# Two of the three weight loads that open the kernel, moved from SyncE's DMA queue to ScalarE's

## The chip, the cores and the metric

The kernel runs on one core of one Trainium2 chip. The metric is the device time of one execution in microseconds. Three runs of the kernel before took 254.72, 254.77 and 254.78 us; the median, 254.77 us, is the time that the prediction starts from.

## The reference

Two attention blocks with 32 heads of width 20 are computed on separate inputs, and their outputs stand side by side. Both inputs x have 2048 rows of 640 columns in bf16. A is a sliding-window softmax attention over the last 256 keys, B is a linear attention.

```
qkv = x @ wqkv                       # 640 x 1920: columns of q, of k, of v
A:  scores = q @ k.T * 20 ** -0.5, kept where 0 <= i - j < 256
    o = softmax(scores) @ v;  out[..., :640] = o @ wo
B:  pq, pk = phi(q), phi(k);  phi(t) = (t + 1 if t > 0 else exp(t)) + 1e-6
    kv = pk.T @ v;  z = sum of pk over rows;  o = (pq @ kv) / (pq @ z + 1e-6)
    out[..., 640:] = o @ wo
```

## The kernel before, in words

The 2048 rows are cut into 4 stretches of 512 (SB), each stretch into 4 blocks of 128 (TPS), and the 640 columns into 5 chunks of 128 (KT). A's projections q, k and v of stretch 0 are computed in an opening; then a long loop over the score tiles of A runs, into which a plan written out by hand (lists of due times) fills the matmuls of the later projections, of B and of the output products. The order of instructions on each engine is fixed by the order in which the program issues them (`manual_schedule`); an engine that waits holds up all that stands behind it on that engine.

The change lies in the opening. The first stretch of A's x is not transposed by a DMA. Its rows are loaded as they are into a tile named phi: block 0, block 1, and then blocks 2 and 3 together (`load`, L172 and L173). TensorE turns each block through an identity (`transposes`, L178) into PSUM tiles named first, and DVE (even blocks) or ScalarE (odd blocks) copies the result to xA (L352, L349). The weight columns of v are loaded in three parts along the contraction: chunk 0, chunks 1 and 2, chunks 3 and 4 (`v_parts`, L968), each chunk 160 KB. `v_abreast` then works on all eight products of v (four blocks by two halves) side by side: chunk 0 for the four products of blocks 0 and 1, then the transposes of blocks 2 and 3, then chunk 0 for the other four, then chunks 1 and 2 for all eight, then chunks 3 and 4 (matmuls L411). The raw weight columns of q and k (tiles qpad and kpad, L334, 800 KB each) are regrouped by DVE, ScalarE and GpSimd (`regroup`) into wqk, from which the q rows are computed (L276).

Before any of this is there, TensorE runs dummy products on a zeroed tile (`warm_up`, L196): 18 at once, and 2 more between the transposes of block 0 and those of block 1.

Every load of the kernel before is issued by SyncE (nc.sync), one after the other: block 0, block 1, v chunk 0, blocks 2 and 3, v chunks 1 and 2, v chunks 3 and 4, raw q, raw k, the transposed second stretch of x (xA, L163), B's k weights (wB, L157), and B's first stretch (xB, L163). ScalarE issues no DMA.

Of the kernel before, what the change touches and what calls it, by code (L numbers as in the profile page):

```python
# [21 lines left out]
TPS = SB // P  # L22
# [70 lines left out]
def kernel(  # L93
# [10 lines left out]
    nc = tc.nc  # L104
    _, S, D = A_x.shape
# [35 lines left out]
    w_sb = {}  # L141
# [19 lines left out]
    def load_x(n, s):  # L161
        t = xp.tile([P, KT, SB], BF16, name=f"x{n}")
        nc.sync.dma_start_transpose(out=t[:], in_=xsrc[n][s * SB : (s + 1) * SB, :])  # L163
        return t

    def load_x_first():

        tok = pqp.tile([P, TPS, D], BF16, name="phi")
        src = xsrc["A"][0:SB, :].rearrange("(t p) d -> p t d", p=P)
        t = xp.tile([P, KT, SB], BF16, name="xA")  # L170

        def load(t0, t1):  # L172
            nc.sync.dma_start(out=tok[:, t0:t1, :], in_=src[:, t0:t1, :])  # L173

        def transposes(tb):
            ps = first_ps.tile([P, 2 * SB], BF16, name="first")
            for c in range(KT):
                nc.tensor.transpose(  # L178
                    ps[:, c * P : (c + 1) * P], tok[:, tb, c * P : (c + 1) * P], ident[:]
                )  # L180
            dst = t[:, :, tb * P : (tb + 1) * P]
            pv = ps[:, 0:D].rearrange("p (c q) -> p c q", q=P)

            for c in (slice(0, 2), slice(2, KT)):
                (act_copy if tb % 2 else dve_copy)(dst[:, c, :], pv[:, c, :])

        return t, load, transposes

    def warm_up(wait):

        z = op.tile([P, TPS, D], BF16, name="osb")
        nc.vector.memset(z[:, 0, 0:P], 0.0)
        ps = dps.tile([P, SB], F32, name="dense")
        for n in wait:
            for _ in range(n):
                nc.tensor.matmul(  # L196
                    ps[:, 0:P], lhsT=z[:, 0, 0:P], rhs=z[:, 0, 0:P], start=True, stop=True
                )
            yield
# [45 lines left out]
    load = {"A": 0, "D": 0}  # L245
# [82 lines left out]
    def load_raw(i):  # L328

        pl, name = ((qp, "qpad"), (kp, "kpad"))[i]  # L330
        t = pl.tile([P, NG, SB], BF16, name=name)
        raw = t.rearrange("p g q -> p (g q)")[:, 0 : KT * D].rearrange("p (k n) -> p k n", n=D)
        wv = A_wqkv.rearrange("(kt p) n -> p kt n", p=P)
        nc.sync.dma_start(out=raw, in_=wv[:, :, i * D : (i + 1) * D])  # L334
        return raw
# [12 lines left out]
    def act_copy(dst, src):  # L348
        nc.scalar.activation(out=dst, in_=src, func=ACT.Copy)  # L349
# [610 lines left out]

    v_parts = ((0, 1), (1, 3), (3, KT))
    wv = A_wqkv.rearrange("(kt p) n -> p kt n", p=P)
    load_tokens(0, 1)
    load_tokens(1, 2)
    for k0, k1 in v_parts:
        if k0 == 1:
            load_tokens(2, TPS)
        nc.sync.dma_start(out=w_sb["A"][:, k0:k1, :], in_=wv[:, k0:k1, 2 * D : 3 * D])  # L968
    raw = [load_raw(i) for i in range(2)]
    xA[1] = load_x("A", 1)  # L970
    load_w("B", B_wqkv, 1, nc.sync)
    xB[0] = load_x("B", 0)
    dummies = warm_up((18, 2))
    for tb in range(2):
        next(dummies)
        transposes(tb)
    v_tok[0] = v_bufs[0]
    for i, _ in enumerate(v_abreast(xA[0], v_tok[0], by_tokens, v_parts)):
        if i == 3:
# [191 lines left out]
```

## Time and profile before

The profiled execution took 255.21 us, of which the span from the first to the last instruction is 253.5 us; the median of the runs shown is 254.77 us, 0.44 us below the profiled one.

| what | value |
|---|---|
| TensorE matmul busy | 242.4 us, 96% of the span |
| ScalarE busy | 196.8 us, 78% |
| GpSimd busy | 186.3 us, 73% |
| VectorE busy | 169.5 us, 67% |
| DMA | 37.04 MB, all of the kernel's own transfers on one queue (q1) |

Times in the profile's rows are microseconds from the start of the span. SPq is SyncE's sequencer issuing DMAs; a DMA's row in a timeline is the time that its issue takes and not that of the transfer. In a chain of waits, a row of a DMA reaches from its issue to its landing.

### The profile page before, as it was taken

How to read it: one execution, taken by the hardware profiler on the slowest of the kernel's cores; microseconds unless marked ns; L12 is line 12 of the kernel's file. 1: busy time of each engine (PE TensorE's matmuls, PEld its weight loads, DVE VectorE, ACT ScalarE, POOL GpSimd, SP SyncE). 2: the span in 40 equal slices, each digit the busy share in tenths (PEclk: the TensorE clock that was granted, in tenths of full speed). 3: DMA queues.
4: the chain of work that ended last, by engine and by line, in shares of the span. 5: the costliest groups of instructions: out<-in, count | busy, mean ns of one | idle time of the engine just before them, and what ended most of it. 6: DMA issues, size and time to landing. Idle time of an engine off the chain costs nothing.

```text
span 253.5 us, 8721 instructions
## 1 busy us (share of the span) xinstructions
PE 242.4 (96%) x3677; PEld 141.2 (56%) x3723; DVE 169.5 (67%) x311; ACT 196.8 (78%) x194; POOL 186.3 (73%) x310
## 2 busy tenths in 40 slices
PE   7999999999999999999999999999999999999994
PEld 5644446556755546457445555556455465655573
DVE  1264777767754565767664867677889779859662
ACT  3366788898767788997657888889988899999541
POOL 1125798878787798687778969889877978999800
PEclk9999999999999999999999999999999999999999
DMA  6997699897764252994559495525969956494614
GB/s 195 329 263 152 113 188 109 104 288 192 98 119 28 44 193 41 226 291 127 88 106 185 110 199 117 140 34 86 186 104 171 182 89 168 93 181 101 193 58 153
DMA packets 68396, 37.04 MB, mean 146 GB/s; under 512 B 51589, under 2 KB 67333, under 8 KB 68357
## 3 DMA queue, kind: packets, MB, share of 16 engines
q1 hardware_dynamic: 68357, 36.49, 68.5%
q8 instruction: 29, 0.48, 0.7%
q14 instruction: 10, 0.08, 0.1%
HBM read 14.42 MB, written 9.83 MB: 96 GB/s over the span
## 4 chain that ended last, share of the span: by engine, by line
PE 80%; ACT 6%; issue 5%; DVE 4%; DMA 2%; POOL 1%; SPq 0%; ACTq 0%
PE dense L276 46%; PE S_ps L784 10%; PE dense L559 8%; PE dense L831 7%; PE dense L411 5%; ACT p L792 4%; DMA phi<-in_A_x_dram 2%; ACT e L286 1%; DVE phi L293 1%; PE first L411 1%; POOL p L807 1%; PE dense L713 1%; DVE e L290 1%; DVE tok L749 1%; PE dense L642 1%
## 5 line engine op out<-in xcount | busy, mean ns | idle before, releaser
L807 POOL TENSOR_SCALAR_AFFINE_SELECT p<-p 128x256 bf16<-128x256 bf16 (+2 forms) x280 | 176.5, 660 | 43.3 <-ACT p L792 41.8
L792 ACT ACTIVATE p<-S_ps 128x2048 bf16<-128x2048 f32 x76 | 142.9, 1880 | 33.6 <-PE S_ps L784 29.4
L276 PE MATMUL dense<-xA,wqk 128*128 128x512 bf16 x188 | 48.9, 380 | 1.4 <-issue 1.0
L784 PEld LDWEIGHTS <-kpad 20*128 20x128 bf16 (+1 forms) x1216 | 21.9, 98 | 29.5 <-issue 25.5
L784 PE MATMUL S_ps<-qpad,kpad 20*65 20x64 bf16 (+3 forms) x1216 | 33.7, 227 | 0.3
L844 DVE STREAM_TRANSPOSE T<-dense 128x512 f32<-128x512 f32 x32 | 22.8, 713 | 15.7 <-PE dense L831 15.3
L290 DVE TENSOR_SCALAR e<-e 128x512 bf16<-128x512 bf16 x40 | 18.4, 459 | 20.5 <-ACT e L286 20.5
L293 DVE SCALAR_TENSOR_TENSOR phi<-dense,e 128x512 bf16<-128x512 f32 x40 | 27.7, 692 | 1.6
L276 PEld LDWEIGHTS <-wqk 128*128 128x128 bf16 x200 | 17.9, 98 | 19.2
L831 PE MATMUL dense<-p,vA 128*32 128x64 bf16 (+2 forms) x1216 | 25.9, 231 | 0.6 <-ACT osb L261 0.4
L276 PE MATMUL dense<-wB,xB 128*128 128x128 bf16 (+1 forms) x155 | 25.3, 297 | 0.5 <-issue 0.3
L276 PE MATMUL dense<-xB,wB 128*128 128x512 bf16 x90 | 24.6, 380 | 0.6 <-issue 0.3
L276 PE MATMUL dense<-wo,oT 128*128 128x512 bf16 (+4 forms) x161 | 24.5, 293 | 0.6 <-DVE phi L293 0.3
L559 PE MATMUL dense<-tok,phi 128*128 128x129 bf16 (+1 forms) x152 | 24.1, 296 | 0.9 <-issue 0.8
L286 ACT ACTIVATE e<-dense 128x512 bf16<-128x512 f32 x40 | 23.6, 600 | 1.4 <-PE dense L276 0.8
L411 PE MATMUL dense<-wA,xA 128*128 128x320 bf16 x140 | 24.0, 304 | 0.2 <-issue 0.2
L276 PE MATMUL dense<-wB,xA 128*128 128x128 bf16 (+1 forms) x153 | 22.9, 296 | 0.6 <-issue 0.5
L831 PEld LDWEIGHTS <-vA 128*32 128x32 bf16 x1216 | 19.4, 97 | 4.2 <-issue 1.3
L261 ACT ACTIVATE osb<-dense 128x512 bf16<-128x512 f32 (+2 forms) x28 | 15.8, 578 | 5.7 <-PE dense L276 5.5
L411 PEld LDWEIGHTS <-xA 128*128 128x128 bf16 x160 | 14.9, 98 | 8.5 <-ACT xA L349 0.8
L749 DVE TENSOR_TENSOR tok<-tok,rden 128x640 bf16<-128x640 bf16 x16 | 18.3, 1141 | 0.2 <-issue 0.2
L861 DVE TENSOR_TENSOR N<-T,recA 128x320 bf16<-128x320 f32 (+1 forms) x28 | 16.1, 574 | 3.4 <-DMA oT<-N 2.5
(66 smaller groups left out, 196.8 us busy)
## 6 DMA issues: line engine op xcount, KB each, us to landing
out_dram<-osb SPq DMA_DIRECT2D x7, 640.0 KB
x_scr<-xB SPq DMA_DIRECT2D x4, 640.0 KB
tok<-in_B_x_dram SPq DMA_DIRECT2D x4, 640.0 KB
xB<-x_scr SPq DMA_DIRECT2D x4, 640.0 KB
wB<-in_B_wqkv_dram SPq DMA_DIRECT2D x3, 800.0 KB
q_scr<-qpad SPq DMA_DIRECT2D x16, 60.0 KB
k_scr<-kpad SPq DMA_DIRECT2D x16, 60.0 KB
qpad<-q_scr SPq DMA_DIRECT2D x16, 60.0 KB
```

The lines of the kernel that those rows point to most:

```text
L276: nc.tensor.matmul(dst, lhsT=lhs(kt), rhs=rhs(kt), start=(kt == 0), stop=(kt == KT - 1))
L286: nc.scalar.activation(out=view(e), in_=src, func=ACT.Exp)
L290: nc.vector.tensor_scalar(out=e[:], in0=e[:], scalar1=1e-6, scalar2=1.0 + 1e-6, op0=ALU.add, op1=ALU.min)
L293: nc.vector.scalar_tensor_tensor(out=dst, in0=src, scalar=0.0, in1=view(e), op0=ALU.max, op1=ALU.add)
L411: nc.tensor.matmul(ps[:, 0 : hh * DH], lhsT=xt[:, kt, tb * P : (tb + 1) * P], rhs=w_sb["A"][:, kt, i * hh * DH : (i + 1) * hh * DH], start ...
L559: nc.tensor.matmul(out, lhsT=pk[:, tb, c * P : (c + 1) * P], rhs=x[:, tb, lo:hi], start=(i == 0), stop=(i == len(blocks) - 1),)
L749: nc.vector.tensor_tensor(out=vh, in0=vh, in1=rden_of[s][:, tb, :, :].to_broadcast([P, H, DH]), op=ALU.mult)
L784: nc.tensor.matmul(S_ps[0:keys, j, col : col + n], lhsT=k_pad[kb // TPS][rows, g, ko : ko + keys], rhs=q_pad[s][rows, g, q0 : q0 + n], sta ...
L792: nc.scalar.activation(out=p, in_=S_ps[:], func=ACT.Exp, scale=scale)
L807: nc.gpsimd.affine_select(out=dst, in_=v, pattern=[[0, 4], [0, n], [sgn, w]], compare_op=ALU.is_ge, fill=0.0, base=base, channel_multiplie ...
L831: nc.tensor.matmul(O_ps[32 * j : 32 * (j + 1), q0 : q0 + n], lhsT=v_flat[kb // TPS % 3][:, at + j * HV : at + j * HV + 32], rhs=p[:, j, co ...
L844: nc.vector.transpose(out=T.rearrange("p b e -> p (b e)"), in_=O_ps[:])
```

## The change

The loads of v's chunks 1 and 2 and of chunks 3 and 4 are issued by ScalarE (nc.scalar) and no longer by SyncE. SyncE issues block 0, block 1, v chunk 0, blocks 2 and 3, and then at once raw q, raw k and the rest in the order they had. Ahead of ScalarE's two DMAs stands a copy of one element per partition within the zeroed tile (`act_copy(z[:, 1, 0:1], z[:, 0, 0:1])`), and ahead of that copy ScalarE's function table load. `warm_up`, which holds the copy, is started ahead of the loads in the program; the order of instructions on TensorE and on VectorE is the same as before. `load` takes the issuing engine as an argument, and gets nc.sync each time.

```diff
-        def load(t0, t1):
-            nc.sync.dma_start(out=tok[:, t0:t1, :], in_=src[:, t0:t1, :])
+        def load(t0, t1, eng):
+            eng.dma_start(out=tok[:, t0:t1, :], in_=src[:, t0:t1, :])
...
         nc.vector.memset(z[:, 0, 0:P], 0.0)
+        act_copy(z[:, 1, 0:1], z[:, 0, 0:1])
...
-    load_tokens(0, 1)
-    load_tokens(1, 2)
-    for k0, k1 in v_parts:
-        if k0 == 1:
-            load_tokens(2, TPS)
-        nc.sync.dma_start(out=w_sb["A"][:, k0:k1, :], in_=wv[:, k0:k1, 2 * D : 3 * D])
+    def load_v(part, eng):
+        k0, k1 = part
+        eng.dma_start(out=w_sb["A"][:, k0:k1, :], in_=wv[:, k0:k1, 2 * D : 3 * D])
+
+    dummies = warm_up((18, 2))
+    next(dummies)
+    load_tokens(0, 1, nc.sync)
+    load_tokens(1, 2, nc.sync)
+    load_v(v_parts[0], nc.sync)
+    load_tokens(2, TPS, nc.sync)
+
+    load_v(v_parts[1], nc.scalar)
+    load_v(v_parts[2], nc.scalar)
     raw = [load_raw(i) for i in range(2)]
     xA[1] = load_x("A", 1)
     load_w("B", B_wqkv, 1, nc.sync)
     xB[0] = load_x("B", 0)
-    dummies = warm_up((18, 2))
-    for tb in range(2):
-        next(dummies)
-        transposes(tb)
+    transposes(0)
+    next(dummies)
+    transposes(1)
```

## The prediction

> **What bounds the kernel now.** First the page: the busy times and the chain that ended last say which engine carries the end.
>
> ```profile
> PE 242.4 (96%) x3677; PEld 141.2 (56%) x3723; DVE 169.5 (67%) x311; ACT 196.8 (78%) x194; POOL 186.3 (73%) x310
> PE 80%; ACT 6%; issue 5%; DVE 4%; DMA 2%; POOL 1%; SPq 0%; ACTq 0%
> ```
>
> TensorE is the bound: 96% busy, 80% of the chain. DMA has 2% of the chain, about 4.3 us, and all of it is one transfer. The chain in order of time shows which:
>
> ```profile
> 2.19 4.26 DMA phi<-in_A_x_dram
> 6.45 0.05 issue
> 6.50 0.75 PE first L178 x10
> 7.25 0.02 issue
> 7.27 0.77 ACT xA L349 x2
> 8.04 0.04 issue
> 8.08 0.30 PE first L411
> ```
>
> So the start hangs on blocks 2 and 3 of x: issued at 2.19, landed at 6.45. The transposes and ScalarE's copies follow, and from 8.08 TensorE runs without a hole. In the waits of TensorE after 8.1 us there is no DMA at all; the longest single one is 0.4 us (ScalarE's copy of an output). What the landing loses or gains is therefore handed to the end one for one. The timeline shows what TensorE and the two issuing engines do around it:
>
> ```profile
> 0.80 1.28 ACT L349 ACT_TABLE_LOAD   x1 [0.80 <-PEq L1155]
> 2.19 0.43 SPq L173 DMA_DIRECT2D phi<-in_A_x_dram  x1
> 2.66 0.98 SPq L968 DMA_DIRECT2D wA<-in_A_wqkv_dram  x2
> 4.25 1.40 PE L411 MATMUL dense<-wA,xA 128*128 128x320 bf16 x4
> 4.49 0.77 ACT L349 ACTIVATE xA<-first 128x256 bf16<-128x256 bf16 x2 [2.40 <-PE first L178]
> 6.50 0.73 PE L178 MATMUL first<-ident,phi 128*128 128x128 bf16 x10 [0.86 <-DMA phi<-in_A_x_dram]
> ```
>
> TensorE has done its last piece at 5.64 and stands for 0.86 us. The loads that are moved are issued right behind the one it waits for. Last, the windows of one microsecond, for the DMA (last two columns: busy share of the 16 engines, GB/s):
>
> ```profile
> 2.00:3.00 1.00, 1.00 (x12) 0.91 (x10) 0.00 (x0) 0.09 (x1) 0.00 (x0) 1.00 0.93 273
> 3.00:4.00 1.00, 1.00 (x12) 0.93 (x11) 0.26 (x2) 0.00 (x0) 0.00 (x0) 1.00 0.96 224
> 4.00:5.00 1.00, 1.00 (x8) 0.47 (x6) 0.29 (x2) 0.51 (x2) 0.00 (x0) 1.00 0.77 232
> 5.00:6.00 1.00, 0.64 (x2) 0.05 (x2) 0.00 (x0) 0.25 (x1) 0.00 (x0) 1.00 0.98 338
> 6.00:7.00 1.00, 0.50 (x9) 0.51 (x10) 0.01 (x1) 0.00 (x0) 0.00 (x0) 1.00 1.08 350
> 7.00:8.00 1.00, 0.89 (x8) 0.28 (x5) 0.54 (x2) 0.73 (x2) 0.00 (x0) 1.00 0.96 326
> 8.00:9.00 1.00, 0.93 (x8) 0.68 (x7) 0.00 (x0) 0.03 (x1) 0.00 (x0) 1.00 1.05 385
> ```
>
> The DMA engines are busy almost throughout: the opening is short of bandwidth, not of issues. With 0.033 MB before 2.0, the bytes moved by 3, 4, 5, 6, 7, 8 and 9 us are 0.306, 0.530, 0.762, 1.100, 1.450, 1.776 and 2.161 MB. In the order of issue the loads end at these sums: block 0 0.164, block 1 0.328, v chunk 0 0.492, blocks 2 and 3 0.819, v chunks 1 and 2 1.147, v chunks 3 and 4 1.475, raw q 2.294, raw k 3.113. The sum 0.819 is passed at 5.17 us, and the load lands at 6.45: 1.28 later, since the slowest of the 16 engines decides. For raw q it is 9.37 against 10.41, where GpSimd's wait for it ends: 1.04 later. A landing is thus the time of its sum plus 1.0 to 1.3 us.
>
> **The change part by part.** *The copy of one element* on ScalarE starts after the table load, at 2.08. The nearest rows are its smallest copies of the opening, 0.33 us (128x160). ScalarE had nothing to do until 4.49. *The two DMAs* cost ScalarE what SyncE paid, 0.98 us, so about 2.4 to 3.4: done before 4.49, cost nothing. If they ended after 4.49, the copies of block 1 would be late, and behind them the third and fourth v product; these are covered by TensorE's wait for blocks 2 and 3.
>
> *SyncE* loses two issues. The issue of blocks 2 and 3 stays at 2.19: nothing in front of it has gone. Behind it, raw q moves from 3.69 to 2.66, raw k from 4.20 to 3.18, the transposing load of xA from 4.77 to 3.74, and wB's and xB's follow if the line of bytes lets them. This gains nothing on the path: raw q is passed at the sum 2.294 with the same bytes ahead of it, and wB and xB, issued at 12.79 and 13.42, meet their first user on TensorE only at 28.0.
>
> *The order of the bytes* is the real edit. Before, 0.819 MB go first, and v's 0.655 MB stand behind them on the one queue. Now v's parts stand at the head of a second queue and are worked off beside the first. SyncE's first issue at 0.81 brings bytes at about 1.8, 1.0 later; so ScalarE's at 2.4 brings them at 3.4, when 0.396 MB are moved and 0.423 MB of SyncE's remain up to the end of blocks 2 and 3. The trace has one queue only, so how two share the engines has no row. The ends: SyncE's queue keeps its place (nothing goes ahead, +0, and with the lag of raw q in place of 1.28 even -0.24); or all of v goes ahead: the sum to pass is 1.474, at 7.07, and +1.9. I take equal shares, as both queues ask the same busy engines all the time: 0.423 of v's go with 0.423 of SyncE's, the sum to pass is 1.242, at 6.41, and with raw q's lag of 1.04 (one DMA in a steady stream, as this will be) blocks 2 and 3 land at 7.45, 1.0 us later. With the old lag it is 1.24.
>
> [...]
>
> *What else moves with it.* v chunk 0 shares too: 0.096 MB of it are left at 3.4, the sum 0.588 is passed 0.42 later, and the four products at 4.25 end by 6.06 and not 5.64: hidden, as the wait reaches to 7.45. v chunks 1 and 2 pass at about 6.4 at the latest and land by 7.7; TensorE asks for them after the four chunk 0 products of blocks 2 and 3, then at 9.2 (8.22 plus 1.0). v chunks 3 and 4: all 0.655 MB shared, sum 1.706, passed at 7.8, landed by 9.1; asked for at 11.4. Raw q lands at 10.4 as before, and DVE takes it up behind v's products, at 11.8 plus 1.0. All hidden.
>
> The sum: +1.0 on the landing, 0 for the rest. In the profiled execution of before, 255.21 us (span 253.5), that makes 256.2; against the median of the runs, 254.77, which is 0.44 lower, **255.8 us**. Shares from equal to most to v, and lags of 1.04 to 1.28, make the likeliest case 255.4 to 256.4.
>
> **The rivals.**
>
> *A: v's loads come too late to matter much.* Condition: ScalarE's issue starts not at 2.4 but towards 4. For it: ScalarE's next row after the table load is at 4.49, so the trace doesn't show how soon it is free; against: nothing stands between. With an issue at 3.8, bytes come at 4.8, when 0.716 MB are moved and 0.103 remain; the sum 0.922 is passed at 5.47, +0.3, a little more where slow engines have more left: about +0.4, 255.2, within 0.2%. The same place is reached if the engines stay with SyncE's queue (+0).
> [...]
>
> *B: faster, since a second queue fills the slack of the engines.* Place: the windows from 3 to 5 us, where they move 224 and 232 GB/s and later 338 to 385. If those are waits of single transfers that another queue's can fill, the rate from 3.4 on is 385: with equal shares 0.846 MB take 2.2 us, to 5.6, and if the lag, then no longer made by stalls, is 0.3, the landing is at 5.9, 0.55 earlier: 254.2. The turning point: share and rate together must bring it ahead of 6.45, that is a lag under 0.85 even at full rate. TensorE's own work up to 5.64 caps the gain at 0.86 (253.9). Against it: busy shares of 0.96 and 0.77 in these windows leave little to fill.
>
> *C: TensorE falls back to its slow pace.* It did 5 transposes in 0.71 us at 2.99 and 10 in 0.73 at 6.50. Its hole would grow from 0.86 to about 1.8 us, and what comes behind could run at the early pace for a microsecond or two: +1.0 more, 256.8. Against it: after the hole of 0.86 it was at full pace.
>
> *D: nothing changes* beyond the issuing queue, as every load of v is hidden before and after: covered by A's +0.
>
> **How the numbers follow.** 0.2% is 0.51 us, about what a measurement of this kernel can tell from no change. The forecast has 0.58 (255.4 to 256.4), C and other large losses 0.07, A and D 0.16, B 0.19. Slower by over 0.2% takes the forecast and C: 0.65; within it A and D and the mild end of B: 0.17; faster the rest of B: 0.18. For 8 in 10 the range runs from the middle of B's 253.9 to 254.26, about 254.1, to the forecast's upper end, 256.4.
>
> **What the profile after will show.** ScalarE's two issues at about 2.4 to 3.4 (A: near 4). A second hardware queue with 0.66 MB. The chain's DMA row ending at about 7.45 and not 6.45, the ten transposes at 7.5, and TensorE without a hole from about 9.1, every later row about 1.0 later. The waits of TensorE still with blocks 2 and 3, now 1.5 to 1.8 us, and none for v. The prediction is wrong if those blocks land before 6.9 (then look at the rates from 3 to 5 us, B, or at a late issue, A), or if TensorE waits for v's parts or raw q, which would mean that the second queue is served far less than half.

## The result and the profile after

The changed kernel takes 257.0 us (median of 6 runs, 256.61 to 257.51) against 254.78 us for the kernel before (median of 6 runs, 254.72 to 255.97). The ratio is 1.0064, with a 95% interval of 1.0038 to 1.0091. So it is slower, by 2.2 us by the medians and by 1.6 us by the ratio. The forecast was 255.8 us with a range of 254.1 to 256.4: the direction was right, the size was not, and the time lies above the range. The changed kernel was run twice more, on other chips, with 1.0063 and 1.0071. The profiled execution shown here took 256.73 us, with a span of 255.0 us (before: 253.5).

The page of the profile after: busy times, the DMA queues (packets, MB, share of the 16 engines' span), and the chain that ended last.

```profile
PE 248.0 (97%) x3723; PEld 141.4 (55%) x3723; DVE 168.1 (66%) x311; ACT 196.9 (77%) x195; POOL 186.8 (73%) x310
q1 hardware_dynamic: 67813, 35.83, 65.7%
q10 hardware_dynamic: 544, 0.66, 0.8%
PE 88%; DVE 3%; ACT 3%; DMA 2%; issue 2%; SPq 0%; POOL 0%; ACTq 0%
```

TensorE is still the bound. There is a second hardware queue, q10, with v's 0.66 MB, as the diff says. The chain in order of time (start, length, what):

```profile
2.19 4.92 DMA phi<-in_A_x_dram
7.11 0.05 issue
7.15 1.04 PE first L178 x10
8.19 1.28 PE first L412 x4
9.47 1.82 PE dense L412 x8
...
14.55 5.40 PE dense L277 x25
```

The same pieces in the chain of before:

```profile
8.38 1.09 PE dense L411 x8
...
12.73 0.22 PE dense L276
```

Blocks 2 and 3 of x land at 7.11, 0.66 later than before (6.45). But the first q product, the last row, stands at 14.55, and before it was at 12.73: 1.82 later. So the landing is only the smaller part of the loss. The chain shows the rest: the ten transposes take 1.04 (0.75 before) and the eight v products 1.82 (1.09 before), with no wait between. The timeline shows ScalarE and TensorE (in brackets the idle time before, and what ended it):

```profile
0.80 1.28 ACT L350 ACT_TABLE_LOAD   x1 [0.80 <-PEq L1162]
1.04 0.95 ACTq L966 DMA_DIRECT2D wA<-in_A_wqkv_dram  x2
2.10 0.20 ACT L350 ACTIVATE osb<-osb 128x1 bf16<-128x1 bf16 x1
...
4.90 0.45 PE L178 MATMUL first<-ident,phi 128*128 128x128 bf16 x5 [0.82 <-DMA phi<-in_A_x_dram]
6.25 0.70 PE L412 MATMUL dense<-wA,xA 128*128 128x320 bf16 x4 [0.90 <-DMA wA<-in_A_wqkv_dram]
7.15 1.04 PE L178 MATMUL first<-ident,phi 128*128 128x128 bf16 x10 [0.20 <-DMA phi<-in_A_x_dram]
...
9.26 2.03 PE L412 MATMUL dense<-wA,xA 128*128 128x320 bf16 x8
```

Two things are to be seen. First, ScalarE issues its two DMAs from 1.04 on (the single rows start at 1.04 and 1.51), in the midst of the table load of 0.80 to 2.08 and ahead of the one-element copy at 2.10, which stands before them in the program. So v's 0.66 MB do not come in behind the x blocks, but among the very first of them. In the window from 3 to 4 us the two queues moved (packets, MB, share of the 16 engines):

```profile
q10 hardware_dynamic: 228, 0.27, 76.0%
q1 hardware_dynamic: 63, 0.08, 21.7%
```

From 2.75 to 3.5 us it was 141 packets of ScalarE's queue and 1 of SyncE's: block 0 was through, and v's chunks 1 and 2, issued at 1.04, went ahead of block 1, issued at 1.25. Second, TensorE now has three waits in place of one: 0.82 for block 1, 0.90 for v chunk 0, 0.20 for blocks 2 and 3. The landings, each the last of the 16 engines, from the semaphore events of the two traces:

| load | before | after |
|---|---|---|
| block 0 | 2.94 | 3.11 |
| block 1 | 3.68 | 4.85 |
| v chunk 0 | 4.18 | 6.21 |
| blocks 2 and 3 | 6.45 | 7.11 |
| v chunks 1 and 2 | 7.28 | 4.42 |
| v chunks 3 and 4 | 8.11 | 6.11 |
| raw q | 10.36 | 9.42 |
| raw k | 12.58 | 11.64 |

What TensorE needs first comes later, and what it needs last comes earlier. After the change the landings follow the order of issue over both queues: block 0 (0.81), v chunks 1 and 2 (1.04), block 1 (1.25), v chunks 3 and 4 (1.51), v chunk 0 (1.72), blocks 2 and 3 (2.19). The windows of one microsecond (busy time of PE, PEld, DVE, ACT, POOL, which are TensorE's matmuls and weight loads, VectorE, ScalarE and GpSimd, with the number of instructions; then TensorE's granted clock as a share of full speed, the DMA share and GB/s):

```profile
3.00:4.00 1.00, 1.00 (x9) 0.67 (x7) 0.09 (x1) 0.00 (x0) 0.00 (x0) 1.00 0.98 352
4.00:5.00 1.00, 0.18 (x3) 0.11 (x3) 0.46 (x2) 0.00 (x0) 0.00 (x0) 1.00 1.06 376
5.00:6.00 1.00, 0.35 (x5) 0.23 (x5) 0.00 (x0) 0.61 (x2) 0.00 (x0) 1.00 1.07 387
...
7.00:8.00 1.00, 0.85 (x10) 0.77 (x10) 0.31 (x2) 0.00 (x0) 0.00 (x0) 0.71 1.07 366
8.00:9.00 1.00, 1.00 (x5) 0.26 (x4) 0.25 (x1) 0.77 (x2) 0.00 (x0) 0.50 1.08 367
9.00:10.00 1.00, 1.00 (x5) 0.56 (x4) 0.00 (x0) 0.00 (x0) 0.53 (x3) 0.50 1.08 369
10.00:11.00 1.00, 1.00 (x7) 0.56 (x5) 0.00 (x0) 0.00 (x0) 0.58 (x3) 0.58 1.08 342
```

The engines move more than before from 3 to 6 us (352, 376, 387 GB/s against 224, 232, 338). And TensorE's granted clock falls to 0.50: in the trace from 7.43 to 10.84, which is 3.41 us. The hole of 4 to 7 us lies ahead of the fall (TensorE busy for 0.18, 0.35 and 0.70 us of its three windows), and the slow pace comes just when the data is there: five products in each of the windows 8:9 and 9:10, where before there were eight and ten matmuls. The second of these windows before:

```profile
9.00:10.00 1.00, 1.00 (x10) 0.70 (x8) 0.00 (x0) 0.00 (x0) 0.00 (x0) 1.00 1.05 362
```

How the loss is made up in this pair of traces, by the starts of the same weight loads on TensorE: +0.65 at the transposes of blocks 2 and 3, +1.04 at the first of the eight v products at 9.26, growing to +1.82 at the last of them; 0.30 of it is given back between 57 and 66 us, and the spans differ by 1.5.

### The profile page after: what moved, and what is told of

It is laid out like the page before. It is cut to its first block, busy times and chain, and to the rows that moved or that the text cites. A ratio compares the mean times of both kernels' runs of the same rounds, so it can differ in the third digit from the quotient of the medians.

```text
span 255.0 us, 8768 instructions
## 1 busy us (share of the span) xinstructions
PE 248.0 (97%) x3723; PEld 141.4 (55%) x3723; DVE 168.1 (66%) x311; ACT 196.9 (77%) x195; POOL 186.8 (73%) x310
## 4 chain that ended last, share of the span: by engine, by line
PE 88%; DVE 3%; ACT 3%; DMA 2%; issue 2%; SPq 0%; POOL 0%; ACTq 0%
PE dense L277 49%; PE S_ps L785 10%; PE dense L560 9%; PE dense L832 8%; PE dense L412 7%; DMA phi<-in_A_x_dram 2%; ACT p L793 2%; PE first L412 1%; PE dense L714 1%; DVE phi L294 1%; ACT e L287 1%; DVE tok L750 1%; PE dense L643 1%; PE dense L671 1%; ACT osb L262 1%
## 5 line engine op out<-in xcount | busy, mean ns | idle before, releaser
L277 PE MATMUL dense<-xA,wqk 128*128 128x512 bf16 x200 | 50.9, 380 | 0.0
L277 PEld LDWEIGHTS <-wqk 128*128 128x128 bf16 x200 | 17.9, 98 | 19.2
L277 PE MATMUL dense<-xB,wB 128*128 128x512 bf16 x100 | 26.1, 380 | 0.0
L277 PE MATMUL dense<-wB,xB 128*128 128x512 bf16 (+1 forms) x160 | 25.9, 300 | 0.0
L560 PE MATMUL dense<-tok,phi 128*128 128x129 bf16 (+1 forms) x160 | 25.5, 300 | 0.0
L277 PE MATMUL dense<-wo,oT 128*128 128x512 bf16 (+4 forms) x165 | 24.9, 295 | 0.3 <-DVE phi L294 0.3
L277 PE MATMUL dense<-wB,xA 128*128 128x512 bf16 (+1 forms) x160 | 24.1, 299 | 0.0
L277 PEld LDWEIGHTS <-oT 128*128 128x128 bf16 x165 | 13.2, 98 | 8.4 <-issue 0.7
```

The lines of the kernel that those rows point to most:

```text
L277: nc.tensor.matmul(dst, lhsT=lhs(kt), rhs=rhs(kt), start=(kt == 0), stop=(kt == KT - 1))
L560: nc.tensor.matmul(out, lhsT=pk[:, tb, c * P : (c + 1) * P], rhs=x[:, tb, lo:hi], start=(i == 0), stop=(i == len(blocks) - 1),)
```

## The experiments

The questions: is it the place of v's loads in the line of bytes, and their early issue, or the copy and the new order of the program; and how much of the loss is the landing, and how much the pace? All times are medians; "before" is the kernel before on the same chip. One number helps to read all of them, the start of the first q product (the first piece of `dense` L277 in the chain), since the spans follow it:

| run | first q product | span | difference |
|---|---|---|---|
| before | 12.73 | 253.5 | 240.8 |
| after | 14.55 | 255.0 | 240.5 |
| after_again | 14.54 | 255.0 | 240.5 |
| after_third | 14.69 | 255.2 | 240.5 |
| e1_held | 15.97 | 256.9 | 240.9 |
| e1_again | 15.71 | 256.2 | 240.5 |
| e2_more_dummies | 13.69 | 254.2 | 240.5 |
| e2_again | 13.54 | 254.0 | 240.5 |
| e3_last_part | 13.45 | 254.5 | 241.0 |
| e4_blocks | 13.65 | 254.1 | 240.4 |
| e4_again | 12.25 | 252.9 | 240.6 |
| e5_all_sync | 12.49 | 252.9 | 240.4 |
| e7_blocks_dummies | 12.59 | 253.0 | 240.4 |
| e9_few_dummies | 11.75 | 252.2 | 240.4 |

Over 4 us of difference in the opening, the rest of the kernel takes 240.4 to 241.0 us. So nearly all of the difference is made in the opening.

### e1_held and e1_again: ScalarE's issue held behind the copy

The copy writes one column of the tile that the DMA fills, so that the program has the DMA wait for it; in the run the copy ends at 2.31 and the issue starts at 2.33. This is the kernel that the forecast had in mind.

```diff
-        act_copy(z[:, 1, 0:1], z[:, 0, 0:1])
+        act_copy(w_sb["A"][:, 1, 0:1], z[:, 0, 0:1])
```

> ScalarE's two loads are now really held behind the table load: the one-element copy writes into the place that the first of them fills, so they are issued at about 2.35 and not at 1.04. Theory E (they went too early: 0.66 MB shared the engines with every one of SyncE's opening loads, and the holes that this made in TensorE's work put it back to half pace from 7.4 to 10.8): v's bytes start at about 3.4, blocks 2 and 3 have to wait for a sum of 1.24 MB, which at the 370 GB/s that the two queues moved together is passed at 5.7 and lands at about 6.4; block 1 lands at 3.7, v chunk 0 before 4.7; TensorE has no hole over 1 us and keeps its full pace: 254.6 to 255.0 us. Rival F (the forecast's sum: what counts is that v goes ahead of blocks 2 and 3 at all): landing at 7.45, 255.8 us.

Measured: 258.7 us (256.16 to 259.52) against 255.25, ratio 1.0119 (1.0080 to 1.0159). The timeline of e1_held:

```profile
2.10 0.21 ACT L350 ACTIVATE wA<-osb 128x1 bf16<-128x1 bf16 x1
2.33 0.94 ACTq L966 DMA_DIRECT2D wA<-in_A_wqkv_dram  x2
...
8.10 0.73 PE L178 MATMUL first<-ident,phi 128*128 128x128 bf16 x10 [1.75 <-DMA phi<-in_A_x_dram]
```

The issue now starts at 2.33, where the forecast had put it. Block 1 is back at 3.56, v chunk 0 at 5.08. Yet blocks 2 and 3 land at 8.05, later than in the changed kernel, and TensorE waits 1.75 us for them. Both theories missed: holding the issue does not give the time back, and the forecast's own premise does not give the forecast's time. The DMA records and the semaphore events show where. ScalarE's first bytes move at 4.02, 1.69 after its issue and not the 1.0 of the forecast, and by 5 us its queue has moved 0.03 MB. SyncE's queue has moved 0.819 MB, the sum up to blocks 2 and 3, by 6.08, with 0.27 MB of v beside it, where the forecast had 0.423 of v and 6.41. Of the 16 engines, the middle one had its part of blocks 2 and 3 in at 6.20 (5.54 before), the last at 8.05. So the share cost less than was forecast; it is the slowest engine that lies 1.85 behind the middle one, where the forecast had a lag of 1.04 behind the sum. After the hole the clock was at half from 9.65 to 13.06.

Was the late engine chance? The same kernel again, on another chip:

> The held issue once more, since its first profile had the landing of the last of 16 engines at 8.05, 1.85 after their median (6.20). Theory J (equal shares for each engine, and one straggling engine decides, which differs from run to run): median again at about 6.2, last anywhere from 6.6 to 8.1, and times that scatter over 2 us or more, from 255 to 259. Rival K (a second queue that opens while blocks 2 and 3 are under way always slows them like that): last at 7.9 to 8.2 and 258 to 259 us again.

Measured: 257.87 us (257.12 to 259.65) against 255.21, ratio 1.0107 (1.0070 to 1.0145). Blocks 2 and 3 land at 8.27, the middle engine at 6.07; half clock from 8.50 to 11.91. So both traces of this order of issue have the late engine. Why one engine was 1.85 and 2.20 us behind the middle one in them was not settled.

### e2_more_dummies and e2_again: TensorE kept busy in the holes

The changed kernel with 11 dummy products in place of 2 ahead of block 1's transposes, and 10 more behind them. If the pace is the larger part, it must come back, though the bytes come as late as ever.

```diff
-    dummies = warm_up((18, 2))
+    dummies = warm_up((18, 11, 10))
...
     transposes(1)
+    next(dummies)
```

> The changed kernel with its loads as they are, and 19 more dummy products: 9 ahead of block 1's transposes and 10 ahead of the first v products, where TensorE stood idle. Theory E: the landing of blocks 2 and 3 stays at 7.1 (+0.65), but TensorE is at full pace behind it: ten transposes in about 0.73 us and not 1.04, eight v products in 1.25 and not 2.03, and 255.2 to 255.6 us. Rival G (the loss is the late loads alone, and the pace at that time doesn't follow from TensorE's holes): 256.6 to 257.5 us as the changed kernel.

Measured: 255.95 us (255.72 to 257.2) against 255.25, ratio 1.0039 (1.0020 to 1.0058). Blocks 2 and 3 land at 7.41, the clock is full from 4.32 on and stays so; the transposes take 0.73. In microseconds that lies between theory E and rival G; against the kernel before on this chip, +0.70, it is where E had it (+0.4 to +0.8 on 254.78). A second time, on the chip on which the changed kernel was run as well:

> The same loads with 19 more dummy products. Theory E: same landing, but full pace behind it; 0.5 to 1.1 us below the changed kernel of the same chip, and about 1.003 to 1.0045 of the kernel before, which is the late landing alone. Rival G (late loads alone make the whole loss): within 0.3 us of the changed kernel.

Measured: 255.84 us (255.65 to 256.34) against 255.20, ratio 1.0017 (0.9995 to 1.0038). Its timeline:

```profile
7.32 0.72 PE L178 MATMUL first<-ident,phi 128*128 128x128 bf16 x10
8.15 1.04 PE L412 MATMUL first<-wA,xA 128*128 128x320 bf16 x4
9.03 1.25 PE L412 MATMUL dense<-wA,xA 128*128 128x320 bf16 x8
```

The landing (7.24) is as late as in the changed kernel, and the eight v products take 1.25 in place of 2.03. The changed kernel on that chip took 256.89 (after_third, below): the dummies are worth 1.05 us by the medians, and the two intervals (0.9995 to 1.0038, 1.0047 to 1.0094) do not touch. So by the medians more than half of the loss is the pace. By the ratios, 1.0039 and 1.0017 are left of the changed kernel's 1.0063 to 1.0071, which puts the share of the pace between about 0.4 and 0.75. The scatter of the 12 runs was 0.7 us here and 1.5 in e2_more_dummies, against 2.3 in the changed kernel.

### e3_last_part: one part alone

Only v's chunks 3 and 4 go by ScalarE; chunks 1 and 2 are back on SyncE behind blocks 2 and 3.

```diff
-    load_v(v_parts[1], nc.scalar)
+    load_v(v_parts[1], nc.sync)
```

> Half of the change: only v's chunks 3 and 4 are issued by ScalarE, chunks 1 and 2 stand on SyncE's queue behind blocks 2 and 3 as before. Theory E: 0.33 MB go ahead, issued at 1.04; block 1 still lands at about 4.7, v chunk 0 at 5.3, blocks 2 and 3 wait for a sum of 1.15 MB and land at 6.3 to 6.5: 254.8 to 255.4 us if the pace holds, 256 if it falls back. Rival F (each byte ahead costs in proportion): half of the loss, 255.9 us.

Measured: 256.25 us (254.94 to 257.12) against 255.25, ratio 1.0034 (1.0016 to 1.0052). The timeline:

```profile
4.98 0.71 PE L178 MATMUL first<-ident,phi 128*128 128x128 bf16 x5 [0.70 <-DMA phi<-in_A_x_dram]
...
6.68 1.27 PE L178 MATMUL first<-ident,phi 128*128 128x128 bf16 x10
```

This run takes the named cause of the forecast away altogether: blocks 2 and 3 land at 6.23, before the 6.45 of the kernel before, and TensorE no longer waits for them. It is slower all the same. With 0.33 MB of v on the other queue, block 1 lands at 4.93 (3.68 before), though 0.58 MB are moved by 4 us and blocks 0 and 1 are 0.328; and behind this hole TensorE still runs slowly: ten transposes in 1.27, with the first clock change of the trace, to full, only at 8.13. (The clock column shows 1.00 up to the first change, whatever the pace is: in the trace of before it does so where five transposes take 0.71, at 2.99, and the same 1.00 behind the change at 6.09, where ten take 0.73. Ahead of the first change the durations tell the pace.) The time alone would suit rival F as well, half of the bytes for half of the loss; the unhurt landing and the slow products speak for the pace.

### e4_blocks and e4_again: the second queue used for what is needed first

If the engines have slack that a second queue fills, it should carry x: ScalarE gets v chunk 0 and block 3, SyncE blocks 0, 1 and 2, and the other v parts behind.

```diff
+    load_v(v_parts[0], nc.scalar)
     load_tokens(1, 2, nc.sync)
-    load_v(v_parts[0], nc.sync)
-    load_tokens(2, TPS, nc.sync)
+    load_tokens(3, 4, nc.scalar)
+    load_tokens(2, 3, nc.sync)
...
-    load_v(v_parts[1], nc.scalar)
-    load_v(v_parts[2], nc.scalar)
+    load_v(v_parts[1], nc.sync)
+    load_v(v_parts[2], nc.sync)
```

> Not the later weights but the urgent loads are shared out: ScalarE issues v chunk 0 and block 3 of x, SyncE blocks 0, 1, 2 and then all the rest of v in the old order. Theory E (two queues move 350 to 390 GB/s from 3 to 6 us, where one moved 224 to 338, and nothing goes ahead of the urgent 0.82 MB): the sum 0.82 is passed at about 4.4, the last of the blocks lands near 5.1, TensorE hardly waits: 253.9 to 254.3 us. Rival H (the slack from 3 to 5 us belongs to the rows of x themselves and not to the single queue): last block at 6.4, 254.8 us.

Measured: 254.59 us (254.13 to 256.74) against 255.25, ratio 0.9974 (0.9952 to 0.9996): 0.66 below the kernel before on this chip, about what theory E had. The last block of x landed at 5.91 in its profile, which was one of the two long runs of the kernel (255.8 us): the clock rose only at 9.54.

> v chunk 0 and block 3 on ScalarE's queue, once more, to see whether its 0.9974 stands. Theory E: the last block of x lands at 5.3 to 6.0 and not at 6.2 to 6.5, while TensorE's own work at half pace (two sets of transposes, four v products) fills most of what that frees: 0.996 to 0.9995. Rival M (nothing is gained, the 0.9974 was scatter): 0.9995 to 1.001.

Measured: 255.04 us (254.0 to 256.18) against 255.20, ratio 0.9990 (0.9967 to 1.0013). The gain was not confirmed. Here the last block landed at 5.22, 1.2 before the 6.45 of the kernel before, and the clock rose at 6.11. In the chain, the transposes stand behind TensorE's own products now, and not behind a DMA:

```profile
4.97 1.19 PE dense L412 x4
6.16 0.61 PE first L178 x10
```

### after_again and after_third: the changed kernel on two more chips

> The changed kernel once more, beside the others on one chip. Theory E: ScalarE issues at 1.04, blocks 2 and 3 land at 7.0 to 7.4, and in the window of 3.41 us that holds TensorE's two holes (its waits for block 1 and for v chunk 0) it is busy for about half and goes back to half pace for the window after it: 1.5 to 2.3 us above the kernel before. Rival G (the half pace of the first profile was an accident of that run): full pace behind the landing, 0.6 to 1.0 above.

Measured: 257.13 us (256.53 to 258.28) against 255.21, ratio 1.0063 (1.0036 to 1.0091).

> The changed kernel beside the version with more dummy products, on one chip. Theory E: landing at 7.1 to 7.7, and TensorE at half pace for about one window behind it, either fallen back or not yet up, as its two holes leave it busy for about half of the window before: 1.0055 to 1.0085 of the kernel before.

Measured: 256.89 us (255.9 to 258.21) against 255.20, ratio 1.0071 (1.0047 to 1.0094). In both, ScalarE's issue is at 1.04 again, blocks 2 and 3 land at 7.63 and 7.54, v chunk 0 at 6.38 and 6.47. But the clock does not fall here: it has not risen yet. It rises at 10.06 and at 10.45. The timeline of after_again:

```profile
4.87 0.71 PE L178 MATMUL first<-ident,phi 128*128 128x128 bf16 x5 [0.81 <-DMA phi<-in_A_x_dram]
6.42 1.23 PE L412 MATMUL dense<-wA,xA 128*128 128x320 bf16 x4 [0.83 <-DMA wA<-in_A_wqkv_dram]
7.67 1.25 PE L178 MATMUL first<-ident,phi 128*128 128x128 bf16 x10
```

The first q product is at 14.54 and 14.69 all the same. So "falls back" is one of two ways to the same loss; the other is not to have come up.

### e5_all_sync: copy and program order alone

Both v parts issued by SyncE; the copy and the order of the program stay.

```diff
-    load_v(v_parts[1], nc.scalar)
-    load_v(v_parts[2], nc.scalar)
+    load_v(v_parts[1], nc.sync)
+    load_v(v_parts[2], nc.sync)
```

> The moved loads go back to SyncE's queue, behind blocks 2 and 3; the one-element copy and the order of the program stay as changed. Theory E: the copy and the order cost nothing, so this is the kernel before: landing at 6.3 to 6.7, ratio 1.000, within 0.002. Rival L (the copy on ScalarE or the earlier table load costs something): 0.2 us or more above.

Measured: 254.78 us (254.28 to 256.14) against 255.21, ratio 0.9982 (0.9962 to 1.0002). The timeline is that of the kernel before again, with one wait of 0.47 for v chunk 0 and one of 0.64 for blocks 2 and 3:

```profile
6.26 0.73 PE L178 MATMUL first<-ident,phi 128*128 128x128 bf16 x10 [0.64 <-DMA phi<-in_A_x_dram]
```

The copy and the order cost nothing that can be measured. The whole loss comes from the queue. This run also shows how small a gain can be read: its loads go in the order of the kernel before, and its ratio is still 0.9982.

### e7_blocks_dummies and e9_few_dummies: the order of e4 and the pace together

e4 with 10 dummies ahead of block 1's transposes, and then with 6:

```diff
-    dummies = warm_up((18, 2))
+    dummies = warm_up((18, 10))
```

> The version with v chunk 0 and block 3 on ScalarE's queue, and 8 more dummy products ahead of block 1's transposes, where TensorE stood idle from 3.9 to 4.7 and so missed the full pace until 9.5. Theory E: TensorE is busy for over 0.85 of each window of 3.41 us, is at full pace by 4.5 to 8 us, and 253.5 to 254.3 us, 0.3 to 0.7 faster than without the dummies. Rival G (pace not from TensorE's holes): as without them, 254.1 to 254.7.

Measured: 254.78 us (254.38 to 255.41) against 255.21, ratio 0.9983 (0.9965 to 1.0002). Full clock from 5.84. The 253.5 to 254.3 of theory E were not reached, and e5_all_sync, whose loads all go by SyncE, had the same median on the same chip. The dummies hold up block 1's transposes, which its landing at 4.09 would have let start:

```profile
4.01 1.07 PE dense L197 x10
5.08 0.53 PE first L178 x5
```

> The same split of the loads with 4 more dummy products ahead of block 1's transposes, which fill TensorE's hole without holding those transposes up past the landing of block 1 at 4.1 to 4.7. Theory E: full pace by 4.5 to 8 us in nearly each run, 0.995 to 0.9985 and less scatter. Rival M: 0.9995 to 1.001.

Measured: 254.85 us (253.9 to 255.65) against 255.20, ratio 0.9979 (0.9956 to 1.0001). The profiled execution is the shortest of all (253.9 us, span 252.2). Its chain waits for one DMA only, block 0, and for no load behind it:

```profile
0.81 2.43 DMA phi<-in_A_x_dram
...
4.00 0.49 PE dense L197 x6
4.49 0.29 PE first L178 x5
...
5.70 0.57 PE first L178 x10
```

With six dummies the ten transposes begin 0.8 us earlier than before (5.70 against 6.50), and the first q product 0.98 earlier. Over 12 runs, however, the ratio's interval reaches to 1.0001, and e5_all_sync had 0.9982 without any such order, so this is not shown to beat the kernel before.

## Why the prediction was wrong, point by point

**What bounds the kernel** was right: TensorE, and what the opening loses is handed on. The forecast said one for one; +1.82 at the first q product became +1.5 in the span, and the table of 14 executions has a spread of 0.6 us in what follows, over 4.2 us of difference in the opening.

**"The copy of one element on ScalarE starts after the table load", and the two DMAs behind it at "about 2.4 to 3.4": this is the step that failed first.** The copy did start at 2.10, but the issues had been done by then; they start at 1.04. The copy writes another tile, and the DMAs' place behind it in the program did not hold them until it had run (issues at 1.04 and 1.51, copy at 2.10). In e1_held, where the copy writes into the DMA's own tile, the issue came behind it (2.33, copy to 2.31). So the sentence of the opening part that an engine that waits holds up all that stands behind it is too strong for the issue of a DMA. For TensorE the same trace bears it out: the eight products of v's chunks 1 and 2 for blocks 0 and 1 stand behind the transposes of blocks 2 and 3, and TensorE waited 0.20 us for those blocks, up to 7.15, though these chunks had landed at 4.42. The sign named for this step in the forecast, "ScalarE's two issues at about 2.4 to 3.4 (A: near 4)", looked for a late issue; an earlier one was not thought of. This step changed which loads came late; what put the time above the range is the pace, below: the landing was only 0.66 later, which handed on one for one makes 255.4.

**The landing of blocks 2 and 3**, forecast at 7.45, was 7.11 (7.63 and 7.54 in the other two traces): near, but by three errors that cancel. With the issue at 1.04 all of v is ahead of these blocks, so the sum to pass is 1.474 MB and not 1.242, 0.66 later on the curve of before (7.07 against 6.41). The curve itself was faster: by the windows after, 0.220 MB were moved at 3 us, 0.572 at 4, 0.948 at 5, 1.335 at 6, and 1.474 is passed at 6.38, 0.69 sooner than 7.07. And the lag was 0.73, not 1.04. 7.45 + 0.66 - 0.69 - 0.31 is 7.11. (The 1.04 was read from GpSimd's start at 10.41; raw q landed at 10.36, so its lag behind the sum was 0.99.)

**"Equal shares"** did not come true either. They were the author's estimate, and no run shows them. In total both queues had moved about 0.66 MB when v was through, but not side by side: from 2.75 to 3.5 us nearly all packets were ScalarE's (141 against 1), and from 3 to 4 us it had 0.27 MB against 0.08. For blocks 2 and 3 this made no difference, since all of v was ahead of them; for block 1 and v chunk 0 it did. Why one queue stood nearly still in that stretch is open.

**"All hidden" was wrong for v chunk 0, and block 1 was not looked at.** The two landed 2.03 and 1.17 later, and TensorE waited 0.90 and 0.82 us for them. The forecast's sign of being wrong, a wait of TensorE for a part of v, did appear, but not from a second queue that is served too little: chunk 0 is on SyncE's queue, and v's other parts were served ahead of it. Raw q, forecast "as before", came 0.94 sooner, which nobody needed. v's own parts, forecast to land by 7.7 and 9.1, were there at 4.42 and 6.11, 4.8 and 6.1 us before TensorE asks for them (9.26 and 12.21).

**The pace: rival C came true, at a chance of 0.07; leaving it out of the sum is the step that put the time above the range.** Its price was put at 1.0 more and its time at 256.8; in the first trace the pace cost 1.17 (from +0.65 to +1.82), and the time was 257.0. The course that it describes was seen (granted clock 0.50 from 7.43 to 10.84); the chance was wrong. "After the hole of 0.86 it was at full pace" was the evidence against it. But in the trace of before the clock rises at 6.09 and the hole, from 5.64 to 6.50, lies across that instant, so the row said little of what a longer hole does. In the three traces with several changes of the granted clock, these lie 3.41 to 3.42 us apart: at 4.01, 7.43 and 10.84 in after, 6.23, 9.65 and 13.06 in e1_held, 5.08, 8.50 and 11.91 in e1_again. Cut at these instants, the traces fall into stretches; in the others the same length is laid off from the one change, which is the author's choice. Here is TensorE's busy share in each, worked out from its matmul rows, whose ends are modelled:

| run | stretch, busy share, and the pace that followed |
|---|---|
| before | 2.67 to 6.09: 0.87, full; 6.09 to 9.50: 0.83, stays full |
| after | 0.60 to 4.01: 0.87, full; to 7.43: 0.44, **half**; to 10.84: 1.00, full |
| after_again | to 3.23: 0.64, still half; to 6.64: 0.52, still half; to 10.06: 0.99, full |
| after_third | to 3.62: 0.75, still half; to 7.04: 0.50, still half; to 10.45: 1.00, full |
| e1_held | 2.82 to 6.23: 0.85, full; to 9.65: 0.45, **half**; to 13.06: 0.99, full |
| e1_again | 1.67 to 5.08: 0.86, full; to 8.50: 0.26, **half**; to 11.91: 1.00, full |
| e2_more_dummies | 0.91 to 4.32: 0.83, full; to 7.74: 0.78, stays full |
| e2_again | to 3.56: 0.73, still half; to 6.98: 1.00, full; to 10.39: 0.95, stays full |
| e3_last_part | 1.30 to 4.71: 0.82, still half; to 8.13: 0.92, full |
| e4_blocks | 2.71 to 6.12: 0.82, still half; to 9.54: 1.00, full |
| e4_again | 2.70 to 6.11: 0.95, full; to 9.52: 0.95, stays full |
| e5_all_sync | 0.73 to 4.15: 0.91, full; to 7.56: 0.64, stays full |
| e7_blocks_dummies | 2.43 to 5.84: 0.96, full; to 9.25: 0.94, stays full |
| e9_few_dummies | 0.79 to 4.21: 0.89, full; to 7.62: 0.89, stays full |

In this table the pace, where it was half, rose behind every stretch with 0.83 and more, and behind none with 0.82 and less; full pace fell behind those with 0.26, 0.44 and 0.45, and stayed at 0.64, 0.78 and more. The changed kernel leaves TensorE with 0.44 to 0.52 between about 3.5 and 7 us, so in all three of its traces it loses: it falls back, or does not come up until 10. Where the stretches lie against the start of the kernel differs from one execution to the next (the clock first changes at 4.01, 10.06 and 10.45 in the three traces of the changed kernel); that this makes much of the scatter of about 1 to 2 us between runs is argued, not shown.

**Rival A** (late, 255.2) was wrong in the other direction: the issue was early. No run shows the 3.8 that it reckoned with: the issue stands at 1.04, held at 2.33, and the copy, at 2.10, starts 0.02 us after the table load, in the changed kernel as in e1_held.

**Rival B** (faster, 254.2) had its rates: 352 to 387 GB/s from 3 to 6 us, where it asked for 385. But they went to v's parts, which nobody waited for. The x blocks have to be in the line that gains: e4, e7 and e9 do this, with the last block at 5.22 to 5.91, and come out at 0.9974 to 0.9990, which e5_all_sync's 0.9982 does not let us call a gain. **Rival D** is out.

**The range**, in its terms: the upper end of 256.4 is "all of v goes ahead" with the lag of 1.04 (8.11 against 6.45), with all larger losses left out at 0.07; equal shares with the old lag make only 256.0. The lower end of 255.4 follows from none of the shares and lags named, which start at 255.8. What is missing is the term for the pace, which belonged to the likeliest case as soon as a hole of 1.5 to 1.8 us was forecast: e1_held had that hole (1.75) and fell to half. Its size, as what the first q product lost beyond the landing, was 1.17 in after, 1.16 in e1_again and 1.64 in e1_held. With the landing of the first trace, +0.65 and +1.17 make +1.82 at the first q product.

## What to carry to other kernels

In these runs a DMA that ScalarE issued did not wait for the table load and the copy to another tile ahead of it to run (issue at 1.04, load to 2.08, copy at 2.10); a copy into its own tile held it (to 2.33). (The issue at 1.04 comes 0.04 after the end of the memset for which that copy waits, at 1.00, so a wait ahead of it in the program may hold a DMA; no run tries this.) So ask of a load moved to a second queue not what it would pass, but what it will now share the engines with from the first byte on, load by load, and put on that queue what is needed first; here this brought the last block of x from 6.45 to between 5.22 and 5.91, and no time that can be told from e5_all_sync's.

In this opening, which waits for DMAs, TensorE's holes cost twice: the late landing (0.65 in the first trace), and the pace after it (1.17). To look for the same elsewhere, add up TensorE's busy share over stretches of some 3.4 us, the distance of the clock's changes here, and count a forecast hole of half such a stretch, like e1_held's 1.75, as a likely loss of full pace, unless dummies fill it: that is an estimate from these 14 traces, in which a full pace fell at a share of 0.45 and stayed at 0.64, with nothing measured between.

## What the runs showed of the hardware that was not expected

ScalarE's sequencer issued DMAs during the table load: issue at 1.04 and 1.51, load from 0.80 to 2.08.

The load's last engine was up to 2.20 us behind the middle one. For blocks 2 and 3 the distance was 0.21 in the first trace of the changed kernel (6.90, 7.11), 0.68 in the second, 0.91 before (5.54, 6.45), and 1.85 and 2.20 in e1_held and e1_again, where ScalarE's issue stands at 2.33. The cause is open; no run tells it.

The sag of the DMA rate in the opening moved with the order of issue: in the windows from 3 to 6 us, 224, 232, 338 GB/s before, 352, 376, 387 after, and 155, 237, 364 in e1_held. In e1_held ScalarE's queue moved nothing in the first of these windows and 0.03 MB in the second, so there the sag is again that of one queue. What makes the sag is open.
